# Dealing 51 instead of 36 gate/up token steps to the kernel-generation stage of a fused state-space and SwiGLU layer

## The chip, the cores and the metric

The kernel runs on one core of one Trainium2 chip. The metric is the device time of one execution in microseconds (us); the time before is the median of three runs. A core has TensorE (PE), VectorE (DVE), ScalarE (ACT), GpSimd (POOL) and SyncE (SP). Each works through its own instruction stream in order. SP, ACT and POOL issue the DMAs.

## The reference

One layer and all its gradients, in bf16, with L = 2048 tokens, D = 576 channels, N = 128 states per channel and F = 4608 hidden units:

```
xn = layernorm(x)
P  = exp(dt * A[:, :, None] * l)               # D x N x L, complex
K  = einsum("dn,dnl,dn->dl", C, P, dt * B).real
s  = irfft(rfft(pad(xn.T)) * rfft(pad(K))).T[:L] + xn * Dskip
h  = silu(xn @ w1) * (xn @ w3)                 # gate, up: 2048 x 4608
out = x + s * silu(h @ w2)
```

The outputs are `out` and the gradients with respect to every input for a given `grad_out`.

## The kernel before

The forward half is four stages. A prologue does the layernorm and prepares tables. The **kernel-generation stage** (kgen) builds K. The **convolution** transforms K, multiplies spectra and transforms back, giving s. `ffn_output` multiplies h with w2, from which the backward pass starts. Gate and up, h = silu(gate) * up, need nothing from kgen or the convolution, so they are woven into both.

*Kgen* (`ssm_kernel`, `kgen_chunk`, `kgen_sum`) goes through 36 chunks of 16 channels. For each, SP loads the row table `E_l` (384 KB); PE multiplies a selector with the chunk's phase rows `lhs_t` into `et_ps` (8 matmuls); ACT turns those into cosines and sines `cs_k` (4 instructions); DVE makes the products `q_k`, `p_k`, `t_k`, `v_k`; SP stores `q_k` and `p_k` for the backward pass (Q_dram, PZ_dram, 768 KB); PE sums over the states into `kps` (16 matmuls); four small copies put `kps` into `KT`. The phase rows of six chunks are one tile, loaded by six DMAs on SP (L671).

*Gate/up steps* (`ffn_hidden`). There are 72: nine blocks of 512 hidden units by eight pairs of token tiles. A step is 20 matmuls, for two halves q = 0 and 1, into `pg` and `pu` (two PSUM buffers each). ACT makes `s_t` = silu(pg), then `g_t` and `u_t`; DVE multiplies `h_t`. SP stores `h_t`, POOL stores `g_t` and `u_t` (256 KB each). The weights `wmB_w` and `wtail` come over SP. One step runs ahead of kgen (LEAD), 36 beside it, 35 later. For the steps in kgen, `g_t` of q = 1 is cast by DVE (L1079) instead of ACT.

*Convolution* (`conv_half`, twice, for 288 channels each). Each half has four blocks of PE transforms of KT (L852, spectra `kraw`), DVE products of the spectra with `u` (loaded from UH_dram by SP, L963) into `V` (L903 to L912, 128x2304 elements), and four inverse transforms on PE (L887), from which DVE makes `s_t`.

*First products* (`ffn_output`, L1161). PE multiplies transposed hidden tiles with w2: `hcA`, `hcB` and `hcC` are loaded out of H_dram by SP with transposing DMAs (L1712), w2's second part `w2g` by POOL (L1136). `hcB` lies in memory that the convolution used.

What sets the order: every stage is emitted with a due time (`at`), and a scheduler sorts the instructions of each engine by these at build time. `KG = (start, pitch)` gives kgen's times, `gate_time(n)` and `gate_mark(n)` those of step n, and the last argument of `ssm_forward` scales the convolution's. The times are priorities, no more; nothing waits for a clock. Semaphores do the rest. For the DMAs that SP and ACT issue, the program has eight semaphore lanes, taken in turn; a DMA waits until the earlier DMA on its lane is done.

One more name: `odd_grad_out` is a copy of 1152 KB from `grad_out` in device memory to another place there (L593), issued by ACT in the middle of kgen and read only much later.

Of the kernel before, what the change touches and what calls it, by code (L numbers as in the profile page):

```python
# [14 lines left out]
BF16 = mybir.dt.bfloat16  # L15
I32 = mybir.dt.int32
I16 = mybir.dt.int16
P = 128
# [80 lines left out]


class K:
    LEAD, KG = 1, (4, 6.2)

    def __init__(self, tc, aps: dict, dbg: dict | None = None):
        self.tc = tc
# [540 lines left out]
    def ssm_kernel(self, T0, TK, ps, ps1):  # L646
        nc, cfg = self.nc, self.cfg
        D, N = cfg.D, cfg.N
        AV, BV = cfg.AV, cfg.BV
        DC = 16  # L650
        NCH = D // DC
        TW = DC * (AV + BV)
        GE = 6
        assert NCH % GE == 0 and AV == 2 * cfg.LT
        with self.pool(name="kg_l", bufs=2) as lp, \
                self.pool(name="kg_e", bufs=3) as ep, \
                self.pool(name="kg_qv", bufs=4) as qvp, \
                self.pool(name="kg_sb", bufs=2) as sb, self.pool(name="kg_dft", bufs=1) as dp:
            prev = []
            self.marks = []  # L660
            for ch in range(NCH):
                yield T0 + TK * ch
                self.at(T0 + TK * ch)
                if ch in (20, 24):
                    self.dft_kernel_matrices(dp, (ch - 20) // 4)
                if ch % GE == 0:
                    LT_ = lp.tile([P, GE, N], BF16, name="lhs_t")
                    nc.gpsimd.memset(LT_[:], 1.0)
                    for k in range(3):
                        for q, r0 in enumerate((0, 64)):  # L670
                            nc.sync.dma_start(out=LT_[r0 + k * DC:r0 + (k + 1) * DC],  # L671
                                              in_=self.PCS_dram[q, k, ch * DC:(ch + GE) * DC, :].rearrange(
                                                  "(k p) n -> p k n", p=DC))
# [52 lines left out]
    def kgen_sum(self, ch, qv, ps1, T, TK):  # L726
        nc, cfg = self.nc, self.cfg
        DC, AH = 16, cfg.AV // 2
        q, v = qv
        kps = ps1.tile([P, DC // 2, 4 * AH], FP32, name="kps")  # L730
        self.at(T - 30)
        for j in range(DC // 2):
            for k in range(2):
                with self.tc.issue_after(self.tail.ins):
                    nc.tensor.matmul(kps[:, j, :], lhsT=q[:, k, 2 * j:2 * j + 2].rearrange("p h s i -> p (h s i)"),
                                     rhs=v[:, k, 2 * j:2 * j + 2, :].rearrange("p h a -> p (h a)"), start=(k == 0), stop=(k == 1))
        d1 = 8 * (ch % 9)
        self.at(T + TK)
        KT = self.KT[:].rearrange("p a (g h d) -> p a g h d", g=4, h=2)[:, :, ch // 9, :, d1:d1 + 8]
        for h in range(2):  # L740
            for hf in range(2):
                copy = nc.vector.tensor_copy if (h, hf) == (1, 1) else nc.scalar.copy
                copy(out=KT[64 * hf:64 * hf + 64, :, h],
                     in_=kps[64 * h:64 * h + 64, :, (2 * h + hf) * AH:(2 * h + hf + 1) * AH].rearrange("p j a -> p a j"))

# [245 lines left out]
    def gate_time(self, n):  # L991
        if n < self.LEAD:
            return 4.3 * n
        i = n - self.LEAD
        return self.KG[0] + 2 + self.KG[1] * i if i < 36 else self.KG[0] + self.KG[1] * 36 + 2 + 5.2 * (i - 36)

    def gate_mark(self, n):
        i = n - self.LEAD
        if i < 36:
            return i - 1  # L1000
        h, k = divmod(i - 36, 18)
        return 36 + 8 * h + (-1, -1, 0, 0, 1, 1, 2, 3, 3, 3, 4, 4, 4, 5, 5, 5, 6, 6)[k]

    def ffn_hidden(self, wp, gup):
        nc, cfg = self.nc, self.cfg
# [11 lines left out]
        for fb in range(F // FB):  # L1017
# [14 lines left out]
            for n in range(LT // NT):  # L1032
# [16 lines left out]
                for q in range(NT):  # L1049
# [23 lines left out]
                    puv = pu[:].rearrange("p (g f) -> p g f", g=ng)  # L1073
                    with self.tc.issue_after(self.exps_last.ins):
                        nc.scalar.activation(out=s_t[:, :, q, :], in_=pgv, func=ACT.Silu)  # L1075
                    if step >= self.LEAD + 36 or q == 0:
                        nc.scalar.copy(out=g_t[:, :, q, :], in_=pgv)  # L1077
                    else:
                        nc.vector.tensor_copy(out=g_t[:, :, q, :], in_=pgv)  # L1079
# [942 lines left out]
def kernel(  # L2022
# [35 lines left out]
    with k.ctx:  # L2058
        k.setup_consts()
        k.persist = k.ctx.enter_context(tc.tile_pool(name="persist", bufs=1))  # L2060
        k.dram = k.ctx.enter_context(tc.tile_pool(name="scratch_dram", bufs=1, space=bass.MemoryType.DRAM))
        k.ffn_scratch()
        mats = ExitStack()
        matp = mats.enter_context(k.pool(name="mats", bufs=1, side="right"))
        wtctx = ExitStack()
        k.wtp = wtctx.enter_context(k.pool(name="wt", bufs=1, side="right"))
        with k.pool(name="xT", bufs=1) as xp, k.pool(name="kg_sel", bufs=1) as selp, \
                k.pool(name="f_w", bufs=2) as wp, k.pool(name="f_gu", bufs=3) as gup, ExitStack() as fctx:
            gate = k.ffn_hidden(wp, gup)
            k.prologue(matp, selp, xp, gate)  # L2070
            ktctx = ExitStack()
            k.ktp = ktctx.enter_context(k.pool(name="s_kt", bufs=1, side="right"))
            k.fps = fctx.enter_context(k.pool(name="f_ps", bufs=2, space=bass.MemoryType.PSUM))
            k.ssm = k.ssm_forward(*k.KG, 1)
            for _ in gate:
                pass
        gctx = ExitStack()
        gop = gctx.enter_context(k.pool(name="go_keep", bufs=1))
        k.go_o = gop.tile([P, k.cfg.LT, k.cfg.D], BF16, name="go_o")
        k.gop = gop  # L2080
        goT = gop.tile([P, k.cfg.DT, k.cfg.L], BF16, name="goT")
# [35 lines left out]
```

## Time and profile before

| | |
|---|---|
| three runs | 1782.29, 1785.68, 1786.62 us; median 1785.68 |
| profiled execution | 1790.74 us, span 1788.5 |
| mean granted PE clock | 0.98 |
| PE / DVE / ACT / POOL busy | 92% / 76% / 51% / 20% of the span |
| kgen | 106.4 to 363.9 us |
| convolution | 363.9 to 545.0 us |
| second round of hcA products | from 601.73 us |

The profiled execution is one run; the span is what the profiler saw from first to last instruction. Stages are cut where PE begins the first matmul of the next. In rows of the timeline, the bracket is the idle time ahead of the instruction on its engine and what ended it. In rows of the waits, the numbers are the total, how many times, and the longest.

### The profile page before, as it was taken

How to read it: one execution, taken by the hardware profiler on the slowest of the kernel's cores; microseconds unless marked ns; L12 is line 12 of the kernel's file. 1: busy time of each engine (PE TensorE's matmuls, PEld its weight loads, DVE VectorE, ACT ScalarE, POOL GpSimd, SP SyncE). 2: the span in 40 equal slices, each digit the busy share in tenths (PEclk: the TensorE clock that was granted, in tenths of full speed). 3: DMA queues.
4: the chain of work that ended last, by engine and by line, in shares of the span. 5: the costliest groups of instructions: out<-in, count | busy, mean ns of one | idle time of the engine just before them, and what ended most of it. 6: DMA issues, size and time to landing. Idle time of an engine off the chain costs nothing. (4 is left out here: it accounts for less than half of the span.)

```text
span 1788.5 us, 35198 instructions
## 1 busy us (share of the span) xinstructions
PE 1638.1 (92%) x13765; PEld 1199.0 (67%) x13765; DVE 1360.2 (76%) x2186; ACT 906.7 (51%) x1688; POOL 356.7 (20%) x587
## 2 busy tenths in 40 slices
PE   6788589999999899899999999999999998799988
PEld 2444244454445677788888888888888776678866
DVE  8768589979582555697877879659999966778656
ACT  5778479886765111775665757465444410001001
POOL 3012122212225111111111111111111233132132
PEclk9989899999999999999999999999999999999999
DMA  8879799978789989758576775679999999999992
GB/s 215 272 251 337 262 325 341 359 267 269 234 262 253 233 213 207 225 175 220 173 203 207 185 214 172 175 196 280 241 251 225 218 253 212 194 236 228 216 210 53
DMA packets 639220, 414.05 MB, mean 232 GB/s; under 512 B 428446, under 2 KB 583822, under 8 KB 634446
## 3 DMA queue, kind: packets, MB, share of 16 engines
q1 hardware_dynamic: 585228, 284.79, 65.2%
q0 software_dynamic: 32208, 109.01, 18.8%
q10 hardware_dynamic: 21618, 18.00, 4.0%
q8 instruction: 108, 1.77, 0.4%
q14 instruction: 58, 0.48, 0.1%
HBM read 130.88 MB, written 191.94 MB: 181 GB/s over the span
## 5 line engine op out<-in xcount | busy, mean ns | idle before, releaser
L1901 PEld LDWEIGHTS <-acts 128*128 128x128 bf16 x2304 | 226.7, 99 | 63.3 <-issue 1.8
L1850 PEld LDWEIGHTS <-xn_bf 128*128 128x128 bf16 x2304 | 224.0, 98 | 43.2 <-issue 17.1
L1435 DVE TENSOR_TENSOR pr_q<-et_ps,pz 128x1024 f32<-128x1024 f32 x144 | 176.0, 1222 | 38.5 <-PE et_ps L1430 27.9
L1901 PE MATMUL px<-wT,acts 128*128 128x288 bf16 x1472 | 195.7, 292 | 1.4 <-DMA wT<-in_B_w_dram 1.4
L1061 PEld LDWEIGHTS <-xnT 128*128 128x128 bf16 x1152 | 108.5, 99 | 127.5 <-issue 30.7
L1438 DVE TENSOR_REDUCE S_all<-pr_q 128x32 f32<-128x1024 f32 x144 | 175.3, 1217 | 3.2
L1789 PE MATMUL ph<-w2T,goT 128*128 128x256 bf16 x1440 | 172.0, 273 | 3.2 <-ACT gh L1792 3.2
L1061 PE MATMUL pg<-wmB_w,xnT 128*128 128x512 bf16 x576 | 157.9, 388 | 3.7 <-ACT g_t L1077 3.7
L1789 PEld LDWEIGHTS <-goT 128*128 128x128 bf16 x1440 | 138.9, 98 | 21.6 <-issue 5.6
L1061 PE MATMUL pu<-wmB_w,xnT 128*128 128x512 bf16 x576 | 151.8, 384 | 0.5 <-DMA wmB_w<-in_B_w_dram 0.5
L1830 PE MATMUL pgw<-go_o,h_n 128*128 128x288 bf16 x1152 | 148.7, 286 | 0.3 <-DVE h_n L1764 0.2
L1850 PE MATMUL pgw<-gu_n,xn_bf 128*128 128x256 bf16 x1152 | 134.5, 273 | 9.9 <-ACT gw L1834 5.9
L1850 PE MATMUL pgw<-gg_n,xn_bf 128*128 128x256 bf16 x1152 | 130.4, 273 | 2.1 <-ACT gw L1852 2.0
L1830 PEld LDWEIGHTS <-h_n 128*128 128x128 bf16 x1152 | 112.2, 98 | 29.6 <-issue 1.8
L1075 ACT ACTIVATE s_t<-pg 128x512 bf16<-128x512 f32 x144 | 87.8, 609 | 73.8 <-PE pu L1069 52.3
L1852 ACT CAST gw<-pgw 128x256 bf16<-128x256 f32 x144 | 52.1, 373 | 142.2 <-PE pgw L1850 142.1
L1901 PE MATMUL px<-wA,acts 128*128 128x288 bf16 x832 | 108.5, 286 | 2.2 <-DMA acts<-GU_dram 1.5
L1792 ACT CAST gh<-ph 128x512 bf16<-128x512 f32 x144 | 81.1, 598 | 55.1 <-PE ph L1789 53.0
L1968 ACT ACTIVATE go<-gx 128x576 bf16<-128x576 f32 x15 | 10.2, 683 | 186.6 <-DVE gx L1949 164.3
L1089 POOL DMA_DIRECT2D G_dram<-g_t x72 | 52.2, 725 | 250.7 <-ACT g_t L1077 138.9
L1083 DVE TENSOR_TENSOR h_t<-s_t,u_t 128x1024 bf16<-128x1024 bf16 x72 | 49.4, 686 | 56.9 <-ACT u_t L1080 35.3
L1080 ACT CAST u_t<-pu 128x512 bf16<-128x512 f32 x144 | 88.2, 612 | 3.3 <-PE pu L1061 2.7
(331 smaller groups left out, 3217.1 us busy)
## 6 DMA issues: line engine op xcount, KB each, us to landing
U_dram<-u_t POOLq DMA_DIRECT2D x72, 256.0 KB, 5.0
G_dram<-g_t POOLq DMA_DIRECT2D x72, 256.0 KB, 4.3
H_dram<-h_t SPq DMA_DIRECT2D x72, 256.0 KB, 4.3
Q_dram<-q_k SPq DMA_DIRECT2D x36, 512.0 KB, 4.2
gg_n<-G_dram POOLq DMA_DIRECT2D x18, 1024.0 KB, 6.3
h_n<-U_dram POOLq DMA_DIRECT2D x18, 1024.0 KB, 8.8
GG_dram<-gg_n SPq DMA_DIRECT2D x36, 512.0 KB, 10.8
GU_dram<-gu_n SPq DMA_DIRECT2D x36, 512.0 KB, 3.8
```

Source lines behind the costliest of these rows:

```text
L1061: ins = nc.tensor.matmul(pt[:], lhsT=xnT[:, c, ts], rhs=wm[w][:, c, :], start=(q == 0 and c == 0), stop=(q == 1 and c == nfull - 1))
L1075: nc.scalar.activation(out=s_t[:, :, q, :], in_=pgv, func=ACT.Silu)
L1080: nc.scalar.copy(out=u_t[:, :, q, :], in_=puv)
L1089: self.u_stores[step] = nc.gpsimd.dma_start(out=dst[fb * ng:(fb + 1) * ng, :, i0:i0 + NT, :].rearrange("g p t f -> p g (t f)"), in_=src[:] ...
L1435: nc.vector.tensor_tensor(out=pr[:].rearrange("p r k e -> p r (k e)"), in0=T[x][:].rearrange("p k z d a -> p (k z d a)")[:, None].to_broad ...
L1438: nc.vector.tensor_reduce(out=self.S_all[:, :, d0:d0 + 4], in_=pr[:].rearrange("p r k (d a) -> p (r k) d a", d=4), op=ALU.add, axis=AX.X)
L1789: self.pe_last = nc.tensor.matmul(ph[j][:, k, :].rearrange("p (a f) -> p a f", f=P), lhsT=lw, rhs=rh, start=(n == 0), stop=(n == nfull))
L1792: self.sc(lambda: nc.scalar.copy(out=gh[:, j], in_=ph[j][:]))
L1830: self.pe_last = nc.tensor.matmul(pgw[pi_][:, 0:pw], lhsT=hn[:, tt, fl * P:(fl + 1) * P], rhs=go_o[:, tt, po:po + pw], start=(tt == 0), st ...
L1850: self.pe_last = nc.tensor.matmul(pw_[:, 0:FG], lhsT=self.xn_bf[:, tt, c * P:(c + 1) * P], rhs=nat[:, tt, :], start=(tt == 0), stop=(tt == ...
L1852: self.sc(lambda: nc.scalar.copy(out=gw[:, c], in_=pw_[:, 0:FG]))
L1901: self.pe_last = nc.tensor.matmul(px[pi_][:, 0:pw], lhsT=acts[i][:, ai, fi, :], rhs=w[:, po:po + pw], start=(n == 0), stop=(n == len(steps ...
```

## The change

- 51 steps in place of 36 beside kgen, 20 in place of 35 later. Kgen's pitch is 7.3 in place of 6.2; the convolution's times are scaled by 0.76; `gate_time` and `gate_mark` are rewritten to deal the steps so.
- The phase rows of the next six chunks are loaded at the third chunk of a group, four chunks ahead of their use, in place of at the first chunk that uses them.
- Of the four copies into `KT`, DVE makes two (was one) and ACT two (was three).
- The cast of `g_t` on DVE for q = 1 now holds for 51 steps.
- The due times of `ffn_output` and `backward` are 8 lower.

```diff
-    LEAD, KG = 1, (4, 6.2)
+    LEAD, KG, GK = 1, (4, 7.3), 51
...
+            def load_lhs(c0):
+                t_ = lp.tile([P, GE, N], BF16, name="lhs_t")
+                nc.gpsimd.memset(t_[:], 1.0)
+                for k in range(3):
+                    for q, r0 in enumerate((0, 64)):
+                        nc.sync.dma_start(out=t_[r0 + k * DC:r0 + (k + 1) * DC],
+                                          in_=self.PCS_dram[q, k, c0 * DC:(c0 + GE) * DC, :].rearrange("(k p) n -> p k n", p=DC))
+                return t_
...
                 if ch % GE == 0:
-                    LT_ = lp.tile([P, GE, N], BF16, name="lhs_t")
...
+                    LT_ = ahead if ch else load_lhs(0)
+                elif ch % GE == 2 and ch + GE < NCH:
+                    ahead = load_lhs(ch - 2 + GE)
...
-                copy = nc.vector.tensor_copy if (h, hf) == (1, 1) else nc.scalar.copy
+                copy = nc.vector.tensor_copy if h == hf else nc.scalar.copy
...
-        return self.KG[0] + 2 + self.KG[1] * i if i < 36 else self.KG[0] + self.KG[1] * 36 + 2 + 5.2 * (i - 36)
+        return self.KG[0] + 2 + self.KG[1] * 36 * min(i / self.GK, 1) + 7 * max(i - self.GK, 0)
...
-        if i < 36:
-            return i - 1
-        h, k = divmod(i - 36, 18)
...
+        if i < self.GK:
+            return i * 36 // self.GK - 1
+        h, k = divmod(i - self.GK, 10)
+        return 36 + 8 * h + (-1, 0, 1, 2, 3, 3, 4, 5, 5, 6)[k]
...
-                    if step >= self.LEAD + 36 or q == 0:
+                    if step >= self.LEAD + self.GK or q == 0:
...
-            k.ssm = k.ssm_forward(*k.KG, 1)
+            k.ssm = k.ssm_forward(*k.KG, 0.76)
...
-        k.ffn_output(455, 10)
+        k.ffn_output(447, 10)
...
-        k.backward(675, 36, 90, 15, 18, gctx, mats)
+        k.backward(667, 36, 90, 15, 18, gctx, mats)
```

Line numbers of the changed kernel are 6 higher than before for most of these places (L692 becomes L698); the loads of `lhs_t` go from L671 to L667.

How the order moves, at three places. The first is around the odd_grad copy: SP's queue, before, where the copy is on the lane of the second `wmB_w` load (row 111).

```order
105 L1086 DMA H_dram<-h_t 128x2x512
106 L714 DMA Q_dram<-q_k 128x2048
107 L708 DMA PZ_dram<-p_k 128x1024
108 L671 DMA lhs_t<-PCS_dram 16x6x128 x3
109 L675 DMA E_l<-E_dram 128x1536 x2
110 L86 DMA wmB_w_2709<-in_B_w_dram 128x4x512
111 L86 DMA wmB_w_2711<-in_B_w_dram 128x4x512
112 L86 DMA wtail<-in_B_w_dram 64x512 x2
113 L675 DMA E_l<-E_dram 128x1536
114 L671 DMA lhs_t<-PCS_dram 16x6x128 x6
```

And now, where it is on the lane of the last of the five `lhs_t` loads of row 117; row 118 is the `E_l` of chunk 14, which was row 113.

```order
111 L86 DMA wmB_w_3083<-in_B_w_dram 128x4x512
112 L86 DMA wtail<-in_B_w_dram 64x512 x2
113 L1092 DMA H_dram<-h_t 128x2x512
114 L667 DMA lhs_t<-PCS_dram 16x6x128
115 L714 DMA PZ_dram<-p_k 128x1024
116 L720 DMA Q_dram<-q_k 128x2048
117 L667 DMA lhs_t<-PCS_dram 16x6x128 x5
118 L681 DMA E_l<-E_dram 128x1536
```

The weights moved ahead of the copy, the phase rows of chunks 18 to 23 came into its place, and the same `E_l` still stands behind what waits for it. DVE's order there, before and then now (E_l of chunk 14 is the last of the three in row 244, and row 259):

```order
242 L718 TENSOR_TENSOR t_k<-p_k,WT 128x1024 x2
243 L722 TENSOR_TENSOR v_k<-t_k 128x1024
244 L692 TENSOR_SCALAR E_l<-E_l 128x512 x3
245 L1079 CAST g_t<-pg 128x2x256
246 L1083 TENSOR_TENSOR h_t<-s_t,u_t 128x2x2x256
247 L711 TENSOR_TENSOR q_k<-cs_k,E_l 128x2x16x32 x2
```

```order
257 L749 CAST KT<-kps 64x16x8
258 L728 TENSOR_TENSOR v_k<-t_k 128x1024
259 L698 TENSOR_SCALAR E_l<-E_l 128x512
260 L1085 CAST g_t<-pg 128x2x256
261 L1089 TENSOR_TENSOR h_t<-s_t,u_t 128x2x2x256
262 L717 TENSOR_TENSOR q_k<-cs_k,E_l 128x2x16x32 x2
```

The step's cast and product and chunk 12's products are behind that E_l in both.

The second place is the end of kgen on SP, before and now:

```order
227 L1086 DMA H_dram<-h_t 128x2x512
228 L714 DMA Q_dram<-q_k 128x2048
229 L708 DMA PZ_dram<-p_k 128x1024
230 L1086 DMA H_dram<-h_t 128x2x512
231 L963 DMA u_5047<-UH_dram 128x2x1152
```

```order
237 L720 DMA Q_dram<-q_k 128x2048
238 L714 DMA PZ_dram<-p_k 128x1024
239 L1718 DMA_TRANSPOSE hcA<-H_dram 128x4x128 x5
240 L1092 DMA H_dram<-h_t 128x2x512
241 L1718 DMA_TRANSPOSE hcA<-H_dram 128x4x128 x2
242 L969 DMA u_5631<-UH_dram 128x2x1152
```

Seven of the transposing loads of `hcA` moved ahead of the convolution's first load of u.

The third is the end of the convolution on POOL, which stores g and u of the last steps and loads `w2g`, before and now:

```order
182 L1089 DMA G_dram<-g_t 128x2x512
183 L1089 DMA U_dram<-u_t 128x2x512
184 L1136 DMA w2g_7122<-in_B_w_dram 128x2x576
185 L1089 DMA G_dram<-g_t 128x2x512
186 L1089 DMA U_dram<-u_t 128x2x512
187 L1136 DMA w2g_7122<-in_B_w_dram 128x2x576
```

```order
165 L1159 DMA s_t_7343<-S_dram 128x576
166 L1157 DMA x_t<-in_A_u_dram 128x576
167 L1158 DMA go_t<-in_grad_out_dram 128x576
168 L1585 MEMSET w2r_8903 128x2x64
169 L1585 MEMSET w2r_8904 128x2x64
170 L1142 DMA w2g_7110<-in_B_w_dram 128x2x576 x2
171 L1142 DMA w2g_7113<-in_B_w_dram 128x2x576 x2
172 L1142 DMA w2g_7116<-in_B_w_dram 128x2x576 x2
```

The last step's stores are rows 158 and 159 now, so that all loads of `w2g` stand behind them; before, they stood among the stores of the last five. On PE, the products of `ffn_output` stood between the last two steps, and now all stand behind the last inverse transform. From there on, every engine's order is the same in both kernels.

More of the change, by code (lines that the diff above doesn't have):

```diff
@@ L666, in ssm_kernel @@
                 if ch % GE == 0:
-                    LT_ = lp.tile([P, GE, N], BF16, name="lhs_t")
[L668 to L673, printed above, removed]
+                    LT_ = ahead if ch else load_lhs(0)
+                elif ch % GE == 2 and ch + GE < NCH:
+                    ahead = load_lhs(ch - 2 + GE)
                 E = ep.tile([P, TW + DC * BV // 2], BF16, name="E_l")
@@ L994, in gate_time @@
         i = n - self.LEAD
-        return self.KG[0] + 2 + self.KG[1] * i if i < 36 else self.KG[0] + self.KG[1] * 36 + 2 + 5.2 * (i - 36)
+        return self.KG[0] + 2 + self.KG[1] * 36 * min(i / self.GK, 1) + 7 * max(i - self.GK, 0)
     def gate_mark(self, n):
         i = n - self.LEAD
-        if i < 36:
-            return i - 1
-        h, k = divmod(i - 36, 18)
-        return 36 + 8 * h + (-1, -1, 0, 0, 1, 1, 2, 3, 3, 3, 4, 4, 4, 5, 5, 5, 6, 6)[k]
+        if i < self.GK:
+            return i * 36 // self.GK - 1
+        h, k = divmod(i - self.GK, 10)
+        return 36 + 8 * h + (-1, 0, 1, 2, 3, 3, 4, 5, 5, 6)[k]
     def ffn_hidden(self, wp, gup):
```

## The prediction

> **What bounds the kernel now.** I read the table of busy time by stage first, then the waits of the generation stage, then the timelines around its longest waits, at last the timelines of the convolution and of the first products. Columns of the first fence: stretch, length, busy us (and instructions) of PE, weight loads, DVE, ACT, POOL, then the granted clock, the DMA share and GB/s.
>
> ```profile
> 106.40:363.90 257.50, 218.12 (x1594) 108.65 (x1592) 206.12 (x375) 202.33 (x444) 55.13 (x76) 0.95 0.93 318
> 363.90:548.00 184.10, 176.44 (x1017) 86.98 (x1016) 143.41 (x201) 135.24 (x271) 48.85 (x69) 1.00 0.82 257
> ```
>
> The first row is the generation stage (kgen), the second the convolution with its gate steps. In the convolution PE is busy 96% of the time: it is full. In kgen PE is busy 85%, and at a clock of 0.95. What PE could do there is counted from gapless places:
>
> ```profile
> 450.18 1.03 PE L1061 MATMUL pg<-wmB_w,xnT 128*128 128x512 bf16 x4
> 454.27 1.03 PE L1061 MATMUL pg<-wmB_w,xnT 128*128 128x512 bf16 x4
> 319.91 0.82 PE L697 MATMUL et_ps<-SEL,lhs_t 128*128 128x256 bf16 x6
> 320.56 0.59 PE L1061 MATMUL pg<-wmB_w,xnT 128*128 128x512 bf16 x2
> 321.84 0.63 PE L735 MATMUL kps<-v_k,q_k 128*128 128x64 bf16 x16 [0.68 <-DVE KT L743]
> 322.30 0.38 PE L697 MATMUL et_ps<-SEL,lhs_t 128*128 128x256 bf16 x2
> 322.52 0.60 PE L1061 MATMUL pg<-wmB_w,xnT 128*128 128x512 bf16 x2
> ```
>
> One gate step is 454.27 - 450.18 = 4.09 us. A chunk is 0.65 (319.91 to 320.56) + 0.46 (321.84 to 322.30) + 0.22 (322.30 to 322.52) = 1.33. Kgen holds 37 steps and 36 chunks: 151.3 + 47.9 = 199.2 us. It takes 257.5, so 58.3 are lost. That loss is the room the change moves work into. Its parts (line, awaited work, us in total, times, longest):
>
> ```profile
> DVE E_l L692 <- DMA E_l<-E_dram: 35.3, 13, 9.2
> PE pg L1069 <- DVE g_t L1079: 10.3, 3, 7.2
> PE kps L735 <- DVE KT L743: 9.3, 17, 2.1
> PE et_ps L697 <- ACT cs_k L699: 8.4, 16, 1.9
> PE et_ps L697 <- DMA lhs_t<-PCS_dram: 7.4, 1, 7.4
> PE et_ps L697 <- DMA E_l<-E_dram: 2.3, 1, 2.3
> ```
>
> The five PE rows add up to 37.7; the other 20.6 is half-speed clock and small gaps. The worst place is one copy:
>
> ```profile
> 185.57 0.79 ACTq L593 DMA_DIRECT2D odd_grad_out<-in_grad_out_dram  x1
> 193.82 9.38 SPq L86 DMA_DIRECT2D wmB_w<-in_B_w_dram  x2
> SPq L86 <- DMA odd_grad_out<-in_grad_out_dram: 8.5, 1, 8.5
> 208.85 0.29 DVE L692 TENSOR_SCALAR E_l<-E_l 128x512 bf16<-128x512 bf16 x1 [9.23 <-DMA E_l<-E_dram]
> 209.92 0.58 PE L1069 MATMUL pg<-wtail,xnT 64*128 64x512 bf16 x1 [7.19 <-DVE g_t L1079]
> 190.00:196.00 6.00, 0.00 (x0) 0.00 (x0) 0.00 (x0) 0.51 (x1) 0.72 (x1) 0.94 0.92 305
> 208.00:214.00 6.00, 1.96 (x20) 1.27 (x20) 5.02 (x10) 0.29 (x2) 0.72 (x1) 0.50 0.55 187
> ```
>
> ACT issues the odd_grad copy at 185.57. SP, at 193.82, must put a weight load on the same one of the eight lanes that SP and ACT share, and waits 8.5 us for the copy; the E_l load of chunk 14 is queued behind it. DVE waits for it to 208.85 in front of all its later work, PE waits for DVE's cast, and then runs at a clock of 0.50.
>
> **The change part by part.**
>
> *Steps into kgen.* 52 steps in place of 37: 52 x 4.09 + 47.9 = 260.6 us on PE without loss. Per chunk PE now has 7.2 us. DVE gets 15 more casts and 15 more products h_t, 0.69 each by the rows below, so +20.6.
>
> ```profile
> L1079 DVE CAST g_t<-pg 128x512 bf16<-128x512 f32 x36 | 24.8, 690 | 5.0 <-ACT s_t L1075 4.1
> L1083 DVE TENSOR_TENSOR h_t<-s_t,u_t 128x1024 bf16<-128x1024 bf16 x36 | 24.7, 685 | 1.4 <-ACT u_t L1080 1.4
> L743 DVE CAST KT<-kps 64x128 bf16<-64x128 f32 x34 | 10.0, 294 | 1.1
> ```
>
> *KT copies.* One of four goes from ACT to DVE: 36 x 0.294 = 10.6 us more on DVE. DVE: 206.1 + 20.6 + 10.6 = 237.3 of at least 260.6, so it stays below PE; ACT is lower still. The copy is hidden by that slack. Without it (below) it counts in full.
>
> *Phase rows four chunks ahead.* The six lhs_t loads go onto SP's queue earlier; the wait of 7.4 can go. The stall as a whole does not: in the new order the odd_grad copy stands on ACT behind chunk 11's cs_k, the sixth of those lhs_t loads takes its lane, and chunk 14's E_l load stands directly behind it on SP. DVE still takes that E_l ahead of chunk 12's q_k. I give 3 of the 7.4 back to PE as waiting for DVE.
>
> *Loss of kgen after*, by the rows above: the casts 10.3, unchanged; lhs_t 3; KT waits 5 (from 9.3) and cs_k waits 5 (from 8.4), since each engine beside PE now has about 1 us of slack per chunk; E_l 2; clock and gaps 12 (from 20.6), with one long stall fewer. Sum 37. Bounds: 20 if the E_l stalls go too (5 + 5 + 2 + 8), 58 if nothing shrinks. I take 37, as the two rows with long single waits are tied to DMAs that keep their place. Kgen then ends at 106.4 + 260.6 + 37 = 404.0, against 363.9: 40.1 later.
>
> *Convolution.* 33 steps beside it become 20, and all of them lie ahead of or between its last products.
>
> ```profile
> 363.92 0.65 PE L852 MATMUL et_ps<-KT,dC 128*128 128x288 bf16 x4
> 366.36 0.43 SPq L963 DMA_DIRECT2D u<-UH_dram  x1
> 373.72 1.28 DVE L903 TENSOR_TENSOR V<-k,u 128x2304 bf16<-128x2304 bf16 x1
> L1083 DVE TENSOR_TENSOR h_t<-s_t,u_t 128x1024 bf16<-128x1024 bf16 x31 | 21.2, 685 | 25.8 <-ACT u_t L1080 24.2 <-DMA H_dram<-h_t 1.5
> 542.81 2.19 PE L887 MATMUL et_ps<-V,cT 128*128 128x288 bf16 x16
> ```
>
> PE's own part is 176.4 - 31 x 4.09 = 49.6; with 20.4 steps 133. DVE's is 143.4 - 21.2 = 122 (the h_t row is that of this stage); with 20 steps 136, so DVE becomes the bound. To it come the start, 9.8 us from the first transform (363.92) to the first product V (373.72), which becomes some 14 since SP now issues seven transposes hcA ahead of the first load of u, and 3 for the last inverse transform. Sum 153, against 545.0 - 363.9 = 181: 28 won. Bounds 145 (start as before, part of the DVE work inside it) to 160 (DVE waits for ACT's kraw between halves).
>
> *First products.* Before, five steps and the last loads lay side by side after the last inverse transform; after, no step is left there.
>
> ```profile
> 547.15 13.70 SPq L1712 DMA_TRANSPOSE hcB<-H_dram  x8
> w2g<-in_B_w_dram POOLq DMA_DIRECT2D x10, 288.0 KB, 9.0
> 557.80 4.08 PE L1161 MATMUL po<-w2a,hcA 128*128 128x288 bf16 x32
> 589.30 6.69 PE L1161 MATMUL po<-w2a,hcC 128*128 128x288 bf16 x32 [3.58 <-DMA hcC<-H_dram]
> 601.73 4.08 PE L1161 MATMUL po<-w2a,hcA 128*128 128x288 bf16 x32
> ```
>
> I compare at the second round of hcA, 601.73: 57 us after the last inverse transform (545). The products up to there are 216 matmuls, 27 us at 4.08 per 32. SP can issue hcB only once the last inverse transform has left its memory: 13.7 us for eight, about 1.7 each, and the w2g loads (10, landing 9.0 us after issue) come behind the last stores. The first hcB lands some 10 us in, the ninth at 24, hcC's second half near 28; products wait some 10, and their clock falls as in the 589.30 row, where 32 matmuls took 6.69 in place of 4.08 after a wait of 3.58. Sum 27 + 10 + 2 = 39; bounds 32 to 45.
>
> The Trainium skill (TensorE: Matmul & The Clock Gate, Part 1: The HAM clock gate) says that an idle window of about 3.4 us halves the clock, and that it takes as long of busy time to return. The 208 to 214 row, with 0.50 after 7.19 us of waiting, agrees; by the rule the products would lose about 1.7 us per long wait, an estimate, where I take 2.
>
> *Sum.* The second hcA comes at 404.0 + 153 + 39 = 596.0 in place of 601.73: 5.7 us earlier. From there on the order on every engine is the same, so the shift should carry to the end. The profiled execution took 1790.74 us (span 1788.5), 5.1 above the median of 1785.68; I take the 5.7 off the median: 1780.
>
> **The rivals.**
>
> *A. Kgen fills.* The extra steps cover the E_l waits, the loss falls to 20 to 27, and products take 34 to 39: 10 to 20 more than the forecast, 1760 to 1770. For: most waits on PE are of 0.5 us each (8.4 in 16). Against: the 9.23 us wait in front of DVE's queue, which no PE work covers.
>
> *B. DVE stands for E_l and kgen gets bound there (slower).* DVE's work is 237.3, its other waits 257.5 - 206.1 - 35.3 = 16. Kgen's length by DVE is 253 plus its E_l waits: 288 if they stay at 35.3, under the 297.6 I forecast. They decide from 45 us on; the whole is slower by 5.4 from 56 on. What could bring them there is the transfers:
>
> ```profile
> DMA packets 48101, 81.85 MB, mean 317 GB/s; under 512 B 10047, under 2 KB 29887, under 8 KB 48075
> GB/s 170 242 313 278 363 375 273 297 352 337 371 393 296 306 212 186 224 249 296 329 385 252 367 317 321 262 319 302 399 393 376 336 378 330 260 371 377 388 404 291
> H_dram<-h_t SPq DMA_DIRECT2D x36, 256.0 KB, 4.0
> wmB_w<-in_B_w_dram SPq DMA_DIRECT2D x10, 512.0 KB, 5.6
> ```
>
> A step stores 3 x 256 KB (h, g, u alike) and loads some 0.16 MB: 15 steps add 14 MB, 96 in all. At 317 GB/s that is 303 us, 5 more than the forecast; at 290, 331, and the time would be 1813. Taken at E_l waits of 60 to 65: 1787 to 1800. For: DMA share 0.93 already. Against: slices near 400 GB/s.
>
> The Trainium skill (DMA: Bandwidth & Descriptors, Where 436 GB/s comes from) gives about 358 GB/s as the memory's limit per core; 96 MB would take 268 us by it, an estimate, which speaks against filling kgen below a loss of 8. The slices of up to 404 here lie above that figure.
>
> *C. It cancels.* Loss 40 to 47, or the convolution at 158: within 0.3%, 1781 to 1790.
>
> **How the numbers follow.** The forecast (loss 30 to 40, 1773 to 1783) has 0.42, A 0.20, B 0.23, C 0.15. A time 0.3%, 5.4 us, off is about what a measurement of this kernel can tell from no change. The forecast lies on that line: half of it counts as faster (0.22), half as same (0.20). Faster: 0.22 + 0.20 = 0.42. Same: 0.20 + 0.12 of C = 0.32. Slower: 0.23 + 0.03 = 0.26. The range goes from the middle of A (1764) to the upper end of B's likelier part (1799), leaving about 0.1 on either side.
>
> **What would show it.** Right: first convolution transform near 404, last inverse transform ending near 557, second hcA near 596, an E_l wait of 6 us or more still on DVE around the odd_grad copy, no lhs_t wait on PE, DVE over 85% busy in the convolution, and PE waits for hcB or w2g of 8 us or more after it. Wrong: the transform below 395 (A) or above 412 (B), or a second hcA that is shifted otherwise than the end of the program, which would mean that work behind it is not tied to PE's order.

## The result, and the profile after

The changed kernel takes 1835.67 us (median of 4 runs, 1827.76 to 1845.1) against 1786.15 for the kernel before in the same job: 1.0284 times the time, with a 95% interval of 1.0224 to 1.0343. The profiled execution took 1841.24 us, with a span of 1839.3.

First the table by stage, of the kernel before and of the changed kernel. The columns are those of the prediction's first fence; the stages end at the first transform of the convolution, at the end of the last inverse transform, and at the second round of hcA. Before:

```profile
106.40:363.90 257.50, 218.12 (x1594) 108.65 (x1592) 206.12 (x375) 202.33 (x444) 55.13 (x76) 0.95 0.93 318
363.90:545.00 181.10, 173.44 (x1002) 85.87 (x1001) 141.47 (x198) 135.24 (x271) 47.48 (x68) 1.00 0.82 255
545.00:601.70 56.70, 50.84 (x326) 30.76 (x325) 17.01 (x27) 19.23 (x37) 21.58 (x32) 0.94 1.12 251
```

After:

```profile
106.40:436.40 330.00, 281.63 (x1903) 132.62 (x1902) 236.00 (x441) 237.03 (x485) 77.09 (x106) 0.95 0.85 291
436.40:599.30 162.90, 140.80 (x803) 72.74 (x802) 135.01 (x189) 105.35 (x211) 36.24 (x51) 0.94 0.73 227
599.30:657.20 57.90, 30.32 (x227) 22.69 (x224) 15.02 (x24) 4.71 (x8) 10.96 (x19) 0.76 1.20 196
```

PE does the same work in all three stages together (2922 and 2933 matmuls in the records); only its place changes. So read length minus PE busy, row by row: before 39.4, 7.7 and 5.9 us without a matmul, in sum 53.0; after 48.4, 22.1 and 27.6, in sum 98.1. The idle time of PE did not move to another stage. It grew in all three, by 45.1 us, and the matmuls took 10.4 us longer in sum (442.4 to 452.8), with the clock down to 0.94 and 0.76 in the last two stages. Together that is the 55.5 us by which the second round of hcA came later (601.7 to 657.2). The span grew by 50.8.

Where each stage's idle time comes from. The waits of the generation stage (total, times, longest):

```profile
DVE E_l L698 <- DMA E_l<-E_dram: 47.8, 17, 14.1
ACT KT L749 <- DVE KT L749: 25.1, 22, 3.5
PE et_ps L703 <- ACT cs_k L705: 23.2, 26, 3.4
PE pg L1075 <- DVE g_t L1085: 21.6, 7, 12.1
PE kps L741 <- DVE KT L749: 2.1, 4, 0.8
SPq L1092 <- DVE h_t L1089: 90.3, 39, 6.5
SPq L667 <- DMA odd_grad_out<-in_grad_out_dram: 9.0, 1, 9.0
```

The wait of PE for `lhs_t` is gone, and that for `KT` is down from 9.3 to 2.1. In their place PE waits 23.2 for `cs_k` (before 8.4) and 21.6 for the casts (10.3). DVE's waits for `E_l` rose from 35.3 to 47.8, and a wait is there that the kernel before did not have: the four copies of a chunk go DVE, ACT, ACT, DVE into one tile, and ACT stands 25.1 us behind DVE (before, ACT's waits in front of its `KT` copies were for PE's `kps`, 16.4 us). The odd_grad copy, in the timeline:

```profile
213.75 0.79 ACTq L593 DMA_DIRECT2D odd_grad_out<-in_grad_out_dram  x1
216.90 11.84 SPq L667 DMA_DIRECT2D lhs_t<-PCS_dram  x5
228.78 0.43 SPq L681 DMA_DIRECT2D E_l<-E_dram  x1
231.95 0.29 DVE L698 TENSOR_SCALAR E_l<-E_l 128x512 bf16<-128x512 bf16 x1 [14.13 <-DMA E_l<-E_dram]
232.89 0.58 PE L1075 MATMUL pg<-wtail,xnT 64*128 64x512 bf16 x1 [12.13 <-DVE g_t L1085]
226.00:238.00 12.00, 5.11 (x15) 1.84 (x15) 5.94 (x11) 1.18 (x2) 0.77 (x2) 0.53 0.47 159
```

It is the chain that the order showed: the copy holds the lane of an `lhs_t` load, chunk 14's `E_l` is issued only at 228.78, DVE waits 14.13, PE 12.13, and the clock falls to 0.53. The stall itself did not grow, though. Before, PE waited there 7.19 us for the cast and 2.12 for `KT`, and ahead of both 7.40 for `lhs_t`:

```profile
197.29 1.44 PE L697 MATMUL et_ps<-SEL,lhs_t 128*128 128x256 bf16 x6 [7.40 <-DMA lhs_t<-PCS_dram]
```

From one `v_k` on DVE to the next it was 25.1 us across the copy before, and 19.8 after.

The convolution: first transform, first product V, last inverse transform, and what DVE waits for from the first V to that end.

```profile
436.44 0.65 PE L858 MATMUL et_ps<-KT,dC 128*128 128x288 bf16 x4
451.48 1.36 DVE L909 TENSOR_TENSOR V<-k,u 128x2304 bf16<-128x2304 bf16 x1 [5.78 <-DMA u<-UH_dram]
595.53 3.79 PE L893 MATMUL et_ps<-V,cT 128*128 128x288 bf16 x16 [3.64 <-DVE V L917]
DVE h_t L1089 <- ACT u_t L1086: 4.7, 1, 4.7
DVE k L951 <- ACT kraw L861: 3.7, 1, 3.7
DVE k L954 <- ACT kraw L861: 2.7, 4, 1.1
DVE s_t L981 <- ACT ev L979: 2.4, 4, 1.1
```

The first products, on PE and on SP:

```profile
599.16 4.08 PE L1167 MATMUL po<-w2a,hcA 128*128 128x288 bf16 x32
624.38 6.73 PE L1167 MATMUL po<-w2a,hcB 128*128 128x288 bf16 x32 [21.13 <-DMA hcB<-H_dram]
657.23 5.68 PE L1167 MATMUL po<-w2a,hcA 128*128 128x288 bf16 x32 [6.48 <-DMA hcA<-H_dram]
597.20 5.85 SPq L1718 DMA_TRANSPOSE hcC<-H_dram  x1
603.16 26.28 SPq L1718 DMA_TRANSPOSE hcB<-H_dram  x9
```

PE does 32 products with hcA and then nothing for 21.13 us: one transpose of hcC stands on SP ahead of nine of hcB, which occupy SP for 26.28 us, 2.9 each on the mean; before, eight took 13.70. The mean hides a spread: the first three of the nine took 6.31, 5.85 and 3.94 us, while five loads of `w2g` (issued by POOL from 599.8 to 603.1, landed from 618.1 to 622.4) were under way, and the last six 1.27 to 2.94.

### The profile page after: what moved, and what is told of

Same layout as the page of the kernel before. It is cut to its first block, busy times and chain, and to the rows that moved or that the text cites. A ratio compares the mean times of both kernels' runs of the same rounds, so it can differ in the third digit from the quotient of the medians.

```text
span 1839.3 us, 35209 instructions
## 1 busy us (share of the span) xinstructions
PE 1649.9 (90%) x13765; PEld 1201.4 (65%) x13765; DVE 1379.4 (75%) x2237; ACT 895.7 (49%) x1637; POOL 356.6 (19%) x587
## 5 line engine op out<-in xcount | busy, mean ns | idle before, releaser
L1067 PEld LDWEIGHTS <-xnT 128*128 128x128 bf16 x1152 | 109.5, 100 | 131.5 <-issue 35.3
L1841 POOL DMA_DIRECT2D out_dram<-gw x36 | 20.0, 555 | 333.5 <-ACT gw L1840 230.9
```

What stands on the lines that cost most here:

```text
L1067: ins = nc.tensor.matmul(pt[:], lhsT=xnT[:, c, ts], rhs=wm[w][:, c, :], start=(q == 0 and c == 0), stop=(q == 1 and c == nfull - 1))
```

## The experiments

Ratios are to the kernel before, run on the same chip in the same job.

**The dealing, or the rest?** `after_deal_old` keeps the KT copies and the early phase rows, and deals the steps as before (`gate_time`, `gate_mark` and the other due times too are those of the kernel before):

```diff
-    LEAD, KG, GK = 1, (4, 7.3), 51
+    LEAD, KG, GK = 1, (4, 6.2), 36
...
```

> The changed kernel with the dealing of the steps undone (36 in kgen, pitch 6.2, 35 beside the convolution with the old marks, old due times), so that the phase rows loaded ahead and the KT deal remain. Theory: the loss comes from the dealing (kgen 69 lost, products uncovered), and the phase rows save up to 7 us while the KT deal costs some; time within 10 us of the kernel before (1772 to 1792). Rival: the KT deal alone costs 10 us or more by making ACT wait for DVE: 1792 or above.

Measured 1787.09 us, 1.0021 (0.9992 to 1.0049). Within this interval the whole loss is in the dealing. The KT copies and the early phase rows, put on the old dealing, change nothing that can be measured. `after_again` is the changed kernel once more:

> The changed kernel once more, as the base for the next three. Kgen's end at 425 to 437, the wait for hcB near 20, 2 to 3% slower than the kernel before.

Measured 1821.22 us, 1.0264 (1.0212 to 1.0316). Its generation stage ended at 430.4, its convolution at 591.8 and the second hcA came at 648.1, so profiles of one kernel differ by 6 us at the stage's end and 9 us at the second hcA; a difference below that size shows nothing by itself.

**No step left behind the convolution.** `after_tail5` deals 46 to the generation stage, keeps 20 beside the convolution, and holds five for the first products.

```diff
-    LEAD, KG, GK = 1, (4, 7.3), 51
+    LEAD, KG, GK = 1, (4, 7.3), 46
...
-        h, k = divmod(i - self.GK, 10)
-        return 36 + 8 * h + (-1, 0, 1, 2, 3, 3, 4, 5, 5, 6)[k]
+        return 36 + (-1, 0, 1, 2, 3, 3, 4, 5, 5, 6, 7, 8, 9, 10, 11, 11, 12, 13, 13, 14, 15, 15, 15, 15, 15)[i - self.GK]
```

> The changed kernel with 46 steps dealt to kgen, 20 beside the convolution as now, and 5 held back behind its last inverse transform, as the kernel before had it. Theory 3: the 21.1 us wait for hcB and the 6.5 us wait for hcA came because no step was left to cover the loads; five steps (20.5 us of PE) move from kgen into that gap: kgen 15 to 22 us shorter, the stretch from the last inverse transform to the second round of hcA about as long as now (57 to 60), time 15 to 22 us lower. Rival: the loads start later because the steps' own stores stand ahead of them, and hcB is waited for all the same: the stretch grows by 12 or more, and the time falls by under 10.

Measured 1804.27 us, 1.0117 (1.0068 to 1.0166): more than half of the loss is gone. The table by stage of its trace, and the products:

```profile
106.40:408.60 302.20, 254.79 (x1765) 122.95 (x1798) 228.10 (x431) 223.21 (x459) 69.84 (x96) 0.95 0.88 300
408.60:566.40 157.80, 138.15 (x792) 72.12 (x805) 134.72 (x189) 104.85 (x211) 33.64 (x48) 0.95 0.78 242
566.40:622.30 55.90, 49.03 (x321) 29.75 (x322) 16.48 (x25) 19.23 (x37) 20.91 (x31) 0.97 1.14 244
565.90 23.47 SPq L1717 DMA_TRANSPOSE hcB<-H_dram  x8
589.77 1.15 PE L1166 MATMUL po<-w2a,hcB 128*128 128x288 bf16 x8 [0.97 <-DMA hcB<-H_dram]
```

The last stage is 55.9 us long with five steps in it, 57.9 without them: the five steps, 5 x 4.09 = 20.5 us of PE, cost nothing there, because hcB comes no sooner. Its transposes take 2.9 us each on the mean here too; PE only has something to do, and waits 0.97 for hcB instead of 21.13. The clock there is 0.97 against 0.76. In the generation stage the same five steps cost at least their 20.5 us: its end moved from 430.4 and 436.4 to 408.6.

**The KT copies.** `after_kt` goes back to one copy on DVE and three on ACT.

```diff
-                copy = nc.vector.tensor_copy if h == hf else nc.scalar.copy
+                copy = nc.vector.tensor_copy if (h, hf) == (1, 1) else nc.scalar.copy
```

> The changed kernel with the four KT copies dealt as before (three on ACT, the last on DVE). Theory 1: the new deal DVE, ACT, ACT, DVE makes ACT's copy wait for a DVE copy that stands behind other DVE work (25 us of such waits in the changed kernel); cs_k behind it comes late and PE waits 23 us for cs_k. It expects that wait of ACT on DVE to vanish, PE's wait for cs_k to fall to 12 us or less, kgen 8 to 15 us shorter and the time 8 to 15 us lower than the changed kernel's 1836. Rival: cs_k is late because a chunk now has up to two steps of ACT work ahead of it; then the time stays within 4 us, or rises because PE waits for the DVE copy again (9 us before).

Measured 1831.22 us, 1.026 (1.0218 to 1.0302). The waits of its generation stage:

```profile
DVE E_l L698 <- DMA E_l<-E_dram: 58.1, 22, 14.8
PE pg L1075 <- DVE g_t L1085: 29.1, 8, 12.7
PE et_ps L703 <- ACT cs_k L705: 13.1, 24, 4.1
```

ACT's wait for DVE is gone and PE's for `cs_k` fell by 10.1 us. DVE's wait for `E_l` rose by 10.3, and PE's for the casts by 7.5. The stage ended at 427.4, 3.0 earlier than in `after_again`, which is less than two profiles of one kernel differ: the waits traded places.

**The odd_grad copy.** `before_odd` and `after_odd` were meant to put the copy into the convolution (`conv_half`):

```diff
-            with self.tc.issue_after(self.sin_last.ins):
-                nc.scalar.dma_start(out=self.odd["grad_out"][:], in_=...)
...
+        if h == 0:
+            with self.tc.issue_after(self.dft_last.ins):
+                nc.scalar.dma_start(out=self.odd["grad_out"][:], in_=...)
```

> The kernel before with the odd_grad copy moved to the convolution in the same way. It prices the stall in the kernel before: two PE waits of 7.4 and 7.2 us and half clock, 15 to 20 us by theory 2, so about 1768. If the work behind the stall is bound by something else, it is under 6 us.

> The changed kernel with the odd_grad copy issued in the convolution, behind the first half's transforms, and not in kgen. Theory 2: the one copy costs the changed kernel 17 to 20 us (E_l wait of 14.1 on DVE, 12.1 on PE, half clock after it); the stall goes and the time falls by 13 to 20 us. Rival: the stall is a store or E_l queue that is late anyway; then kgen is shortened by under 6 us, or the copy stalls SP in the convolution by as much.

They did not do that: the scheduler put the copy at the start of ACT's stream, where it held a lane of the prologue, and the first chunk of the generation stage began at 128 us in place of 119. Measured 0.9999 (0.997 to 1.0029) and 1.022 (1.0188 to 1.0252), so they answer only in part: without the copy in it the stage of the kernel before ran from 128 to 359.2, 14 us shorter, and that of the changed kernel to 424.8, 15 us shorter than in `after_again`; 9 of them went to the prologue. So the copy costs the stage about the same in both kernels.

The next two pairs leave the order of all instructions as it is and make the copy smaller, leaving out the rest of its rows: two of its eight blocks are copied (`oddq`), or 32 of the 128 rows of each (`oddp32`).

```diff
-                nc.scalar.dma_start(out=self.odd["grad_out"][:], in_=self.turned(self.aps["grad_out"].flatten_outer_dims()))
+                nc.scalar.dma_start(out=self.odd["grad_out"][0:2], in_=self.turned(self.aps["grad_out"].flatten_outer_dims(), 0, 2))
```

```diff
-                nc.scalar.dma_start(out=self.odd["grad_out"][:], in_=self.turned(self.aps["grad_out"].flatten_outer_dims()))
+                nc.scalar.dma_start(out=self.odd["grad_out"][:, 0:32], in_=self.turned(self.aps["grad_out"].flatten_outer_dims())[:, 0:32])
```

> The kernel before with the odd_grad copy cut to a quarter of its rows (two of eight blocks; the later reads take those rows again, so the odd tokens' gradients are not the reference's). Every engine's order stays word for word. Theory 2: the copy holds its lane for some 4 us in place of 17, so SP does not wait for it; the two long PE waits (7.4 and 7.2) and the half clock go: kgen 12 to 18 us shorter, time 12 to 18 lower. Rival: what stalls is bound elsewhere, under 6.

> The changed kernel with the same cut of the odd_grad copy, order unchanged. Theory 2: the E_l wait of 14.1 on DVE and the 12.1 on PE go, kgen 15 to 22 us shorter. If only the kernel before gains, the stall in the changed kernel has another cause.

> The kernel before with the odd_grad copy cut to a quarter in the other direction: 32 of 128 rows of each of the eight blocks, in place of two whole blocks of eight (left out: the other rows; the odd tokens' go_t come from grad_out in plain order, so those gradients are not the reference's). Theory 2b: the copy of two blocks lasted as long as that of eight (about 15 us of packets in the trace) because the blocks are what is spread over the DMA engines, and each engine still had 128 rows to copy one after the other; 32 rows per engine take about 4 us, so SP no longer waits, the 14.6 us of PE waits go and kgen gets 12 to 18 us shorter, the time 12 to 18 lower. Rival: the copy's 17 us are a fixed latency of ACT's queue in kgen: nothing changes, as with the other quarter.

> The changed kernel with the same cut, every order on PE, DVE and SP unchanged. Theory 2b: chunk 12 to 13 takes 24 us now and 6 to 10 then, kgen 14 to 20 us shorter, time 14 to 20 below the changed kernel's. Rival as above: nothing changes.

A quarter of the bytes in two blocks shortened nothing: SP still waited for the copy, 8.4 us in `before_oddq` and 8.6 in `after_oddq` (8.5 and 9.0 with the whole copy), and the ratios are 0.999 (0.9967 to 1.0013) and 1.0238 (1.019 to 1.0286). A quarter of the rows of each of eight blocks did shorten it. SP's wait, in `before_oddq` and then in `after_oddp32`:

```profile
SPq L86 <- DMA odd_grad_out<-in_grad_out_dram: 8.4, 1, 8.4
```

```profile
SPq L667 <- DMA odd_grad_out<-in_grad_out_dram: 0.6, 1, 0.6
PE pg L1075 <- DVE g_t L1085: 12.3, 7, 5.1
PE et_ps L703 <- ACT cs_k L705: 26.1, 26, 3.2
```

With it `before_oddp32` took 0.9967 (0.9938 to 0.9996) and `after_oddp32` 1.0187 (1.0149 to 1.0225). So three quarters of the copy cost the kernel before 0.3%, some 6 us, by an interval that nearly touches 1. In the changed kernel PE's wait for the casts falls by 9.3 and the stage ends at 425.4, 5.0 before `after_again`; the ratio is 0.8 points below that of `after_again`, with intervals that overlap. The step from `v_k` to `v_k` across the copy falls alike, from 25.1 to 18.2 and from 19.8 to 12.8; with the copy out of the stage (`before_odd`, `after_odd`) it is 11.2 and 6.0, 14 us less in each. The copy is a cause of the loss in both kernels, and does not explain why the changed one is slower.

`before_oddpool` lets POOL issue the copy, `before_oddsplit` cuts it into four of 32 rows behind chunks 9, 11, 13 and 15:

```diff
-            with self.tc.issue_after(self.sin_last.ins):
-                nc.scalar.dma_start(out=self.odd["grad_out"][:], in_=self.turned(self.aps["grad_out"].flatten_outer_dims()))
+            with self.tc.issue_after(self.u_stores[-1].ins):
+                nc.gpsimd.dma_start(out=self.odd["grad_out"][:], in_=self.turned(self.aps["grad_out"].flatten_outer_dims()))
```

```diff
...
+                if ch in (9, 11, 13, 15):
+                    self.conv_loads(el, 1, (9, 11, 13, 15).index(ch))
```

> The kernel before with the whole odd_grad copy issued by POOL at the same place in kgen: nothing is left out. POOL's DMAs have eight lanes of their own, and the next DMA on the copy's lane is a store four steps later, some 25 us, so nobody waits for the copy. If the stall costs the kernel before 12 to 18 us: about 1765 to 1770. Rival: kgen is bound by something else and fills the gap: 1778 or more.

> The kernel before with the copy in four parts in the same way. The stall of chunks 12 and 13 (14.5 and 19.0 us from chunk to chunk where 6.2 is usual) goes: kgen 10 to 18 shorter; 1764 to 1774 against 1782. Rival: each part stalls SP by some us and it stays at 1780.

Both come out slower, by about half a per cent: 1.0061 (1.0036 to 1.0086) and 1.005 (1.0021 to 1.008). On POOL the seventh store behind the copy stands 28.8 us, and the trace shows nothing that it waits for:

```profile
POOL G_dram L1089 <- issue: 28.8, 1, 28.8
```

With the copy cut in four, chunks 9, 11, 13 and 15 took 18.6, 12.0, 13.2 and 12.4 us (from a chunk's first `cs_k` to the next chunk's), and those between them some 5.8. SP waited for a part only once, for 1.5 us, so what stalls these chunks was not found.

**Together.** `combo1` joins the dealing of `after_tail5`, the KT copies as before, and the copy issued by ACT in the convolution. `combo41` deals 41 to the generation stage, 25 beside the convolution and 5 behind, with the KT copies as before and the copy on POOL; `combo41s` is the same with the copy in four parts. In all three the hcA loads are due later, behind step 52 (`combo1`) or 47 in place of 42. `after_two_out` is the changed kernel with the KT copies as before and the copy in four parts.

> 46 steps in kgen, 20 beside the convolution and 5 held back behind its last inverse transform; the odd_grad copy issued by ACT in the convolution behind the first transforms; KT copies as before (one on DVE); the hcA loads tied to steps 52 to 59 in place of 42 to 49, so that u is loaded first. If the causes add up (held back 31, copy 15 to 20, u 6, KT 0 to 8 below the changed kernel's 1836): 1772 to 1785. If they overlap, as they would when kgen is bound by the rate of its transfers (96 MB at about 300 GB/s), it stays at 1790 to 1805.

> 41 steps in kgen, 25 beside the convolution, 5 behind its last inverse transform; odd_grad copy by POOL; KT copies as before; phase rows ahead; hcA loads tied to steps 47 to 54. If the dealing itself is worth something once its three costs (uncovered products, copy stall, KT order) are taken out: 1755 to 1770. If PE's idle time in kgen is no room that steps can use: 1775 or more, no better than the kernel before with the copy moved.

> 41 steps in kgen, 25 beside the convolution, 5 behind its last inverse transform, copy in four parts, KT as before, phase rows ahead, hcA loads at steps 47 to 54. If five more steps fit into kgen's idle time: 5 to 12 below before_oddsplit. If PE's idle time there is no usable room: equal to it or slower.

> The changed kernel with two causes out and nothing left out: the odd_grad copy in four DMAs of 32 rows per block (32 rows per DMA engine, 5 us each) behind chunks 9, 11, 13 and 15, and the KT copies as before. If the copy costs 11 to 20 and the KT order 9 of kgen: kgen ends 20 to 28 earlier than in the base of this job, the time is 18 to 28 lower. The products' wait for hcB stays at 15 to 21. Rival: the two overlap in one slack and kgen ends under 14 earlier.

Measured 1.0084 (1.0052 to 1.0117), 1.0106 (1.0065 to 1.0147), 1.0146 (1.0102 to 1.0191), and for `after_two_out` 1.033 (1.0281 to 1.0379). No dealing with more than 36 steps in the generation stage came to the time of the kernel before, so there is no version here that beats it. Set beside `before_oddpool` and `before_oddsplit`, which treat the copy alike, the generation stage of `combo41` and `combo41s` is 23.5 and 25.1 us longer (counted from each run's first gate product), for five steps of 20.5 us of PE.

`after_two_out` was meant to remove both named causes and ends the stage at 441.3, later than the changed kernel. Since four parts of the copy stall the kernel before as well, it does not test the two causes. Its waits:

```profile
DVE E_l L702 <- DMA E_l<-E_dram: 62.0, 26, 5.9
ACT KT L753 <- PE kps L745: 27.8, 8, 9.1
```

The long wait of 14.1 for `E_l` is gone (longest 5.9), and 26 short ones are there in its place, more in sum.

Of these only `combo1` takes the copy out of the generation stage. Its three stages:

```profile
106.40:387.20 280.80, 249.06 (x1756) 122.67 (x1788) 219.67 (x394) 227.34 (x494) 69.64 (x96) 0.99 0.92 318
387.20:553.30 166.10, 140.27 (x792) 72.40 (x805) 134.65 (x188) 104.97 (x211) 33.65 (x48) 0.95 0.75 234
553.30:618.40 65.10, 51.93 (x321) 30.68 (x322) 16.48 (x25) 19.43 (x37) 20.91 (x31) 0.90 1.15 211
```

Its generation stage, with 47 steps as in `after_tail5`, is 21.4 us shorter. But its convolution is 8.3 and its first products are 9.2 us longer, so that 3.9 us are left at the second hcA. The copy and the later loads of hcA fall into these two stages; which of them costs what no run separates.

**SP's queue.** In the changed kernel SP stands 90.3 us waiting for `h_t`, with the `E_l` loads queued behind. `after_hpool` and `before_hpool` let POOL issue these stores in the generation stage, behind those of `g_t` and `u_t`.

```diff
-                self.h_stores[step] = nc.sync.dma_start(out=self.H_dram[...], in_=h_t[:])
...
+                self.h_stores[step] = (nc.gpsimd if step < self.LEAD + self.GK else nc.sync).dma_start(out=self.H_dram[...], in_=h_t[:])
```

> The changed kernel with the stores of h_t of the generation stage issued by POOL, behind g_t's and u_t's, in place of SP; later steps store over SP as before. In the changed kernel SP stands 90.3 us in 39 waits for DVE's h_t, with the loads of E_l queued behind, and DVE then waits 47.8 us for E_l. Theory 'the queue' (the generation stage's excess loss of about 30 us is E_l held behind the stores on SP): DVE's waits for E_l fall to 20 us or less, the stage ends 15 to 30 us earlier (400 to 421), the time falls to 1.008 to 1.018 of the kernel before. Rival 'the engines' (PE, ACT and DVE hand each other small waits, whatever SP does): E_l waits fall, other waits take their place, the stage ends within 8 us of where it did, the ratio is 1.022 to 1.033. Rival 'POOL': POOL's stores are issued late, buffers of h_t, g_t and u_t come free later, and the stage is longer by 5 us or more.

> The same edit in the kernel before, where SP stands 37.5 us in 19 waits for h_t and DVE waits 35.3 us for E_l. 'The queue': E_l waits fall by 10 us or more and the stage by 4 to 10 us, ratio 0.994 to 0.998. 'The engines': within 0.3%. 'POOL': slower by over 0.3%.

Measured 1.0287 (1.0222 to 1.0351) and 1.0022 (0.9986 to 1.0058). What the queue theory forecast did not come: the stage of the changed kernel ended at 435.5, and the waits are those of after.

```profile
DVE E_l L698 <- DMA E_l<-E_dram: 53.0, 22, 14.5
ACT KT L749 <- DVE KT L749: 25.0, 23, 5.2
PE et_ps L703 <- ACT cs_k L705: 24.4, 27, 3.8
SPq L720 <- DVE q_k L717: 153.4, 34, 10.1
```

SP now waits 153.4 us for `q_k`, whose store stands on it as well; the loads of `E_l` are behind that instead. So the edit did not free these loads. It shows that moving the stores of `h_t` alone wins nothing; whether `E_l` held behind stores sets the length of the stage is not settled by it.

## Why the prediction was wrong

The second hcA was forecast at 596.0 and came at 657.2. The 61 us are three terms.

*Loss of the generation stage: forecast 37, measured 69.4* (436.4 - 106.4 - 260.6); 63.4 in `after_again`. This is the step that failed most. It summed the waits of PE and let them shrink because a chunk got more PE work on the mean. By the same sum the loss was 58.3 before, 60.4 in `after_kt`, 58.4 in `after_oddp32`, 62.1 in `after_tail5` (47 steps, 240.1 of work), 65.7 in `combo41` (42 steps, 219.7), 73.2 in `combo41s`, 74.3 in `after_two_out` and 68.5 in `after_hpool`. (All count the stage from 106.4; the first gate product comes between 105.4 and 109.3 in these runs, so a difference of 3 us shows nothing.) Only with the copy out of the stage was it near the forecast's 37: 40.7 in `combo1`, and 44.1 in `before_odd` and 47.8 in `after_odd`, counted from their own first gate product, as their prologue is longer. But that is no effect of the added steps. It is as low with 37 steps (`before_odd`) as with 47 (`combo1`), and from the one to the other the stage is 38.4 us longer, for ten steps of 40.9 us of PE. So with the copy in the stage or out of it, a step added there cost nearly its whole PE time or more: the 58 us were not room.

The term's parts: casts 10.3 forecast, 21.6 measured, as the wait behind the copy grew from 7.2 to 12.1, while that for `lhs_t` went; `cs_k` 5 and 23.2, of which 10.1 go when ACT no longer stands behind DVE's `KT` copy (`after_kt`); `lhs_t` and `KT` 8 and 2.1; the rest, clock and gaps, 12 and some 22. DVE's busy time, 236.0 for a forecast 237.3, was right, and E_l's wait of 6 us or more around the copy was there with 14.1. ACT, forecast lower still, was busy 237.0.

One premise was off as well. The 7.2 us of PE work per chunk, and with it the slack of about 1 us beside PE, is a mean over chunks that are not alike: the dealing gives 15 chunks two steps and most others one. From one `v_k` to the next, the 19 chunks with one step took 6.2 us (median), with DVE busy 6.0 on the mean, and the 15 with two took 10.7, with PE busy 9.4. In a chunk with one step DVE has the most work and no slack, and PE's idle time there is out of reach of the steps dealt to other chunks. From DVE's 6.0 against PE's 4.09 + 1.33 in 19 chunks this is worth some 11 us, an estimate; no run tested it.

Rival B foresaw the direction and gave 331 us for the stage at 290 GB/s; it took 330.0 at 291. Its mechanism is not shown, though. The DMA share fell from 0.93 to 0.85, `combo1` moved 318 GB/s in this stage with ten steps more than the kernel before, and by B's own sum, 253 plus the 47.8 of `E_l`, the stage would have taken 301. So 291 GB/s was no limit of the transfers; the rate is rather low because the stage is long. The Trainium skill's limit of about 358 GB/s (DMA: Bandwidth & Descriptors, Where 436 GB/s comes from) decided nothing: the stage's mean stayed far below it.

*First products: forecast 39, measured 57.9.* The prediction saw that no step is left there and that hcB can be issued only at the end, and priced the wait at 10 by 1.7 us per transpose, as before. They took 2.9 on the mean, one of hcC stood ahead, and PE waited 21.13, then 6.48 for hcA. `after_tail5` shows the size: five steps there are free. The term fails by its size and by what it was compared with: the stage is as long with five steps as without, so taking them out won nothing.

*Convolution: forecast 153, measured 162.9.* DVE's work, 135.0, and the start, 15.0, are as forecast (136 and 14), and 3.6 of that work lies in the start. From the first V on DVE is busy 131.4 of 147.8 us. It stands 16.5 us, where the sum had 3 for the last inverse transform: 13.5 in the four rows above and 1.3 for PE are waits for ACT and PE, which the sum left at nothing and only its upper bound of 160 allowed for. So DVE was busy 83% of the stage, not the over 85% that was to show the forecast right. In the kernel before DVE stood 33.8 us beside a PE that was busy 96%. Once DVE has the most work, its waits count.

From the second hcA on the order is the same, and the shift carried to the end but for 4.7 of 55.5 us.

What stays open: why the loss of the generation stage is as stubborn as it is. The copy's stall is the one large part that the runs show, some 14 us of the stage in either kernel; the order of the KT copies is a small one, and moving the stores of `h_t` off SP changes nothing. In a chunk, PE, ACT, DVE and SP each wait for another once or more (23.2 and 21.6, 25.1, 47.8 and 90.3 us above), and taking one wait away mostly moved time to the others. That this ring sets the pace of a chunk is the likeliest reading; no run here took it apart. A rival is as open: that the loads of `E_l` come late because they stand on SP behind stores that wait for DVE. Nor did a run test why a transpose of hcB takes 2.9 us on the mean in both changed dealings and 1.7 before; that the loads of `w2g` beside the slow ones are the cause is only a guess.

## What to carry to other kernels

Idle time of an engine is room for more work only if that work would run in it. Here, where several in-order engines wait for each other in every turn, more work lengthened the turns by about its own time, and the old loss stayed on top. Divide work and time by the turns that really got the work, not by the mean turn. Before moving work out of a stage, ask what it covers there: five steps behind the convolution covered most of 21 us of waiting for transposes and made that stage no longer. To read such a change, take length minus busy time stage by stage; the work cancels and what is left is where the time went.

## What the runs showed of the hardware

The time of the odd_grad copy does not go by its bytes. In the kernel before, with 288 KB in two blocks of 128 rows it held SP as long (8.4 us) as with 1152 KB in eight (8.5); with 288 KB in eight blocks of 32 rows SP waited 0.4. The Trainium skill (DMA: Bandwidth & Descriptors, Why a DMA increments its semaphore by 16 and not by 1) says that the outermost dimension of a transfer decides over how many engines it is spread, at most 16. These runs fit that, if each block goes row by row on an engine of its own, so that the rows in a block set the time. No run shows which engines moved it, so this is a reading.

In both runs in which POOL issues this copy, the seventh store behind it on POOL stands with nothing in the trace that it waits for, 28.8 us in `before_oddpool` and 35.9 in `combo41`; in the generation stage of the kernel before every store of POOL that stands waits for DVE or ACT. That the copy holds it back is likely, not shown. POOL, busy 20% of the time, was no free place for the copy.
